# Linear attention and four experts on one core: four more chunks turned without TensorE

## The chip, the cores and the metric

The kernel runs on one core of a Trainium2 chip, in fp32. The time is the device time of one execution in microseconds (us), the median of several runs. A core has five engines with a queue of their own each, which work in order: TensorE (PE: matrix products and transpositions, from on-chip memory SBUF into the 8 banks of PSUM), VectorE (DVE), ScalarE (ACT), GpSimd (POOL) and SyncE (SP), which here only issues DMA transfers. They wait for each other through semaphores. Sixteen DMA engines move the data between DRAM and SBUF, and from DRAM to DRAM.

## The reference

```python
# attention: B=4, H=8, S=768, D=64, block=64; lam: one decay per head
for b in range(S // 64):
    sl = slice(b * 64, (b + 1) * 64)
    qb, kb, vb = q[:, :, sl], k[:, :, sl], v[:, :, sl]
    intra = einsum('bhij,bhjd->bhid', einsum('bhic,bhjc->bhij', qb, kb) * Dmask, vb)
    inter = einsum('bhid,bhde->bhie', qb * lam_pow, kv_state)
    out[:, :, sl] = intra + inter
    kv_state = lam_block * kv_state + einsum('bhsd,bhse->bhde', kb * rev_pow, vb)
x = out.transpose(0, 2, 1, 3).reshape(B * S, H * D)          # 3072 x 512
# four experts: w1 512 x 1024, w2 1024 x 512
p = domain_probs / (domain_probs.sum(-1) + 1e-9)
y = sum(p[:, e:e+1] * (relu(x @ w1[e]) @ w2[e]) for e in range(4))
```

## The kernel before

The 3072 tokens are cut into three groups `g` of 1024, and each group into eight chunks of 128 tokens of one batch entry. Chunks are numbered through: 0 to 7 belong to group 0, 8 to 15 to group 1, 16 to 23 to group 2. In group 1, chunks 8 to 11 are batch entries 0 and 1, chunks 12 to 15 are entries 2 and 3, each with the sequence chunks 2 and 3; group 2 holds the sequence chunks 4 and 5 of all four. A pair of group and expert is a *unit*; twelve units follow each other.

The products with w1 and w2 are done by Strassen's method in the form of Winograd, in two levels: seven products M1 to M7 in place of eight, and within each of them seven again. This needs sums of blocks of x (`x_steps`, `own_x`, `own_x_apart`), of the weights (made by GpSimd, kept in DRAM as `w1_ops`, `w2_sums`, `w2_ops` and read back as `ws_in` and `w2t`), and of the hidden activations (`operands`, `later_operands`).

The main loop runs over the units (`at`), over seven products (`i`) and over eight *slots* (`x`) of a product. In a slot TensorE does a piece of the second product (w2) of this unit, into the banks `q..`, and a piece of the first product (w1) of the next unit, into the banks `g1` and `g3`. Round these pieces everything else is laid out in program order by lists: `lately` (work of the attention for VectorE), `background` (operand sums for VectorE), `own_sums` (sums of x), `adds`, `chores` and `queue` (weight sums on GpSimd and their stores), and `steps`, where the attention of chunks 8 to 23 is placed by `AT`, a list of slot numbers counted through from the loop's start. The functions `tt`, `send` and `vector` keep rough clocks of the engines (`busy`, `moved`, `asked`, `filled`), by which the lists are emptied.

A chunk's attention has these steps. `load_more` loads q and k, `load` v. `turn` brings q and k into the form with the head dimension on partitions. `scores`, at slot `AT`, forms the products of k and q (bank pair `q02`, `q12`) and the new state; `values` of the chunk before, in the same slot, gives that chunk's rows of x, through the score banks `s0` and `s1`. VectorE masks, adds to the state and scales q, by the list `lately`.

There are two ways to turn. On the first, TensorE transposes q and k in eight steps of 128x128 into `s0` and `s1` (line 698), and ScalarE copies both to SBUF (lines 706 and 707). On the second (`comes_across`, `load_across`, `turn_across`), SyncE and ScalarE issue, long before, copies from DRAM to DRAM that move runs of 32 columns into the tensor `across` so that, once loaded, VectorE's transposition of 32x32 blocks (line 678) gives the same form. `bring_across` puts 32 such copies per batch entry into the list `pieces`; `trickle` issues one per slot in the first unit (by SyncE and ScalarE in turn) and one every two slots later on; `load_more` issues what is still missing for its chunk, and then loads. Before the change, the chunks of group 2 go the second way.

A DMA has one of eight semaphores, taken in turn, and the instruction that issues it waits till the last transfer on the same semaphore has landed.

The sums of x for the second unit (`SEQ[1:]`, six times four differences of 128x256) are made in the first unit. `own_x` gives them to VectorE with both operands in SBUF. `own_x_apart`, used before the change for group 2 alone, has ScalarE copy two blocks of 128x256 into a bank first, so that one operand of each difference lies in PSUM; `put_back` then issues the differences.

Of the kernel before, what the change touches and what calls it, by code (L numbers as in the profile page):

```python
# [14 lines left out]
FP32 = mybir.dt.float32  # L15
# [6 lines left out]
def kernel(  # L22
# [36 lines left out]
    C = P  # L59
# [49 lines left out]
    def send(out, in_, by=None):  # L109
        n = 4 * min(packet(out), packet(in_))  # L110
        moved[0] = max(moved[0], now[0]) + 4 * math.prod(out.shape) / n * (9 + n / 25) / 16 / 1714
        if by is None:
            asked[0] = max(asked[0], now[0]) + 0.27
        (by or nc.sync).dma_start(out=out, in_=in_)
# [35 lines left out]
    def where(n):  # L150
        g, x = divmod(n, CPG)
        return (x // 4, x % 4) if g == 0 else (2 * g + x // 2 % 2, 2 * (x // 4) + x % 2)
# [304 lines left out]

    SECOND = NCH - 2  # L460
    across = dram.tile([2, P, NHP, B, 8, 32], FP32, name="across")
    pieces = []

    def bring_across(b):
        for x, of in enumerate((q, k)):
            for y in range(4):
                for ac in range(NHP):
                    src = of[b, 4 * (y // 2) + ac, SECOND * C:, (y % 2) * 32:(y % 2 + 1) * 32]
                    to = across[x, y * 32:(y + 1) * 32, ac, b]
                    pieces.append((b, lambda by, to=to, src=src: send(  # L470
                        out=to, in_=src.rearrange("(t p) d -> p t d", p=32), by=by,
                    )))

    def trickle(m=1, by=None):
        for _ in range(m):
            if pieces:
                pieces.pop(0)[1](by)

    def comes_across(n):
        return where(n)[0] >= SECOND  # L480

    def load_across(n):
        c, b = where(n)
        for x, name in enumerate("qk"):
            t = small(f"{name}x")
            send(
                out=t[:].rearrange("p (h c) -> p h c", c=C),
                in_=across[x, :, :, b, (c - SECOND) * 4:(c - SECOND) * 4 + 4].rearrange("p h t d -> p h (t d)"),
            )
            nat[n, name + "x"] = t  # L490

    def load_more(n):
        if not comes_across(n):
            load(n, "qk")
        else:
            trickle(sum(b <= where(n)[1] for b, _ in pieces))
            load_across(n)
            load(n, "k")

# [125 lines left out]
    def take(queue, force=False):  # L625
        for x, f in enumerate(queue):
            if force or getattr(f, "at", 0) <= now[0] and getattr(f, "can", lambda: True)():
                queue.pop(x)()
                return
# [226 lines left out]
        ))  # L856

    FILL = {1: 18, 2: 43}
    AT = (34, 40, 47, 53, 59, 94, 101, 108, 116, 147, 154, 167, 172, 203, 210, 223)
    steps = []  # L860

    def attention():
# [42 lines left out]
    def later_operands(g, e, m):  # L905

        def step(h, m, a):
            if m == "M4":
                t = h["S2"] = h.pop("S3")
                tt(nc.vector, t[:], a[:], t[:], ALU.subtract)  # L910
            elif m == "M2":
                t = h["S1"] = h.pop("A11")
                tt(nc.vector, t[:], h["S2"][:], t[:], ALU.add)
            else:
                t = h["S4"] = h.pop("A12")
                tt(nc.vector, t[:], t[:], h["S2"][:], ALU.subtract)
                spent(h, "S4")

        def through(hs):
            up = [None] * 4  # L920

            def bring(x):
                up[x] = bank(("q02", "q12")[x % 2], "up")
                nc.scalar.copy(out=up[x][:], in_=hs[x]["A12"][:])

            def less(x):
                t = hs[x]["S4"] = hs[x].pop("A12")
                tt(nc.vector, t[:], up[x][:], hs[x]["S2"][:], ALU.subtract)
                spent(hs[x], "S4")
                if x < 2:  # L930
                    bring(x + 2)

            bring(0)
            bring(1)
            background.extend(lambda x=x: less(x) for x in range(4))

        if m == "M6" and unit_of[g, e] == NEST - 1:
            through([hid[g, e, uu, sj] for sj in (1, 0) for uu in range(2)])
        elif m in ("M4", "M2", "M6"):
            ahead = unit_of[g, e] > 0  # L940
            for by in {"M4": ("M4", "M2")[:1 + ahead], "M2": ("M2",)[ahead:], "M6": ("M6",)}[m]:
                for sj in (1, 0):
                    for uu in range(2):
                        h = hid[g, e, uu, sj]
                        background.append(lambda h=h, by=by, a=h["A22"] if by == "M4" else None: step(h, by, a))
# [598 lines left out]
    def own_x(m, g=0, wait=0):  # L1544

        steps = to_do[m] = []

        def sub(f):
            def step():
                steps.pop()  # L1550
                f()
                if not steps:
                    made.add(("x", g, m))

            steps.append(step)

        for f in x_steps(g, m, nc.vector):
            sub(f)
        own_sums.extend(after(wait, f) for f in steps)
# [202 lines left out]
        lambda: own_weights("M1"), sum_own("S1", "A21", "A22", ALU.add), *w2_steps[0:4], mine["M1"], *w2_steps[4:],  # L1762
        raw["A12"],
    ))
    for b in range(B):
        bring_across(b)
    for m in SEQ0[2:]:
        if m == SEQ0[-1]:
# [42 lines left out]
    for at, (g, e) in enumerate(units):  # L1811
# [14 lines left out]
        for i in range(7):  # L1826
# [36 lines left out]
            turned_back = list(after_last.get(SEQ3[i], ())) if nested and not ahead else []  # L1863
            if at == i == 0:
                for m in SEQ[1:]:
                    own_x(m)
            resting[0] = at == NEST - 1 and i >= 5 or at == NEST and i == 0 or at == NEST - 2 and i == 5
            for x, part in enumerate(order):
                for f in part:
                    if f:  # L1870
                        f()
                now[0] += 1
                put = False
                if nested and ahead:
                    idle[1] = x in (1, 4) and (at - 2 * E + 1, i, x) not in held_at
                    put = put_back()
                added = first_steps.pop((at - 2 * E + 1, i, x), None)
                if added:
                    added()
                all_added(now[0])  # L1880
                if joins and not background:
                    joined()
                elif added and x > 2 or put:
                    pass
                elif (ahead or x % 2 == 0 and x + i) and not (nests and i == 6 and x == 7):
                    if nested or nests:
                        if lately:
                            take(lately)
                        else:
                            rest()  # L1890
                        if at == 2 * E and i in (2, 3) and fits():
                            rest()
                    else:
                        took = False
                        for of in (lately, background, own_sums):
                            if of and (not took or fits() or of is background and len(of) > 4):
                                take(of)
                                took = True
                        if at == 0 and i == 1 and x in (0, 3, 6):
                            take(own_sums)  # L1900
                if nested or nests:
                    take(aside)
                    if own_sums and (nested or fits()):
                        take(own_sums)
                if ending and fits():
                    end_first()
                if nested and ahead and x in (1, 3) and fill3:
                    feed3(*fill3.pop(0))
                if turned_back and x > 0:
                    for y in turned_back.pop(0):  # L1910
                        if SEQ3[i] == END[1]:
                            give(*y[:2], ("s0", "s1"), *y[2:])
                        else:
                            give_across(*y)
                if fill and at * 7 + i >= 6 and x in ((0, 1) if at * 7 + i < 13 else (1, 3, 5) if at * 7 + i == 13 else FEED[nested]):
                    feed(*fill.pop(0))
                while steps and (at * 7 + i) * 8 + x == steps[0][0]:
                    steps.pop(0)[1]()
                if at == 0 or x % 2:
                    trickle(1, nc.scalar if at == 0 and x % 2 else None)  # L1920
                for h in range(1, NG):
                    if x == 3 and 0 <= at * 7 + i - FILL[h] < 7:
                        x_fill(h, SEQ[at * 7 + i - FILL[h]])
                pump(PACE[g])
# [30 lines left out]
```

## Time and profile before

| what | value |
|---|---|
| median of 3 runs (lowest to highest) | 1147.44 us (1145.41 to 1149.49) |
| the profiled execution: its time / its span | 1148.51 us / 1146.7 us |
| mean granted clock of TensorE | 0.999 |
| instructions | 22190 |
| DMA: moved, mean rate | 269.22 MB, 235 GB/s |
| packets: all / under 512 B | 309149 / 141425 |

The span goes from the first to the last instruction. An engine's busy time leaves out its waiting and the issuing of DMAs. In the views, `out<-in` names the tiles written and read; "idle before" is the time that the engine stood still ahead of an instruction, with the one that ended it; a line of code can be that of a helper (117 is `tt`, 114 is `send`). `SPq` rows are DMAs issued by SyncE.

### The profile page before, as it was taken

What the parts mean: (1) busy time and instruction counts of PE and PEld (TensorE: products, weight loads), DVE (VectorE), ACT (ScalarE), POOL (GpSimd) and SP (SyncE); (2) the same over time, 40 slices, a digit from 0 to 9 for tenths busy, and PEclk for the clock granted to TensorE, in tenths of its full rate; (3) what the DMA queues carried; (4) which work ended last, traced back from release to release, by engine and by line L of the source; (5) the groups of instructions that cost most, each with busy time, mean ns of one, the idle gap of its engine ahead of it and who ended that gap; (6) DMA issues with size and microseconds to landing.
All of it is one profiled execution on the core that took longest, in us unless ns stands there. A gap on an engine that the chain in (4) does not pass through costs nothing.

```text
span 1146.7 us, 22190 instructions
## 1 busy us (share of the span) xinstructions
PE 1134.4 (99%) x8015; PEld 989.9 (86%) x8015; DVE 772.9 (67%) x1466; ACT 377.6 (33%) x764; POOL 769.5 (67%) x734
## 2 busy tenths in 40 slices
PE   8999999999999999999999999999999999999998
PEld 7788888888888888888888888888888888888887
DVE  5577876476577748736665566778767576776785
ACT  4322123113312321232344442444345442342332
POOL 2748248645862884853885897895995783873885
PEclk9999999999999999999999999999999999999999
DMA  8785778798999999977767659976679756647552
GB/s 198 169 277 186 192 214 247 253 302 254 304 315 290 280 310 306 299 260 258 244 214 247 199 182 286 339 235 214 207 249 268 225 160 195 201 162 211 173 193 74
DMA packets 309149, 269.22 MB, mean 235 GB/s; under 512 B 141425, under 2 KB 244017, under 8 KB 309041
## 3 DMA queue, kind: packets, MB, share of 16 engines
q1 hardware_dynamic: 291360, 262.66, 74.2%
q10 hardware_dynamic: 17648, 5.15, 2.2%
q8 instruction: 64, 1.05, 0.4%
q14 instruction: 45, 0.36, 0.1%
q0 software_dynamic: 32, 0.00, 0.0%
HBM read 194.83 MB, written 77.10 MB: 237 GB/s over the span
## 4 chain that ended last, share of the span: by engine, by line
PE 94%; DVE 2%; POOL 2%; issue 1%; DMA 1%; ACT 0%; SPq 0%; DVEq 0%; POOLq 0%; ACTq 0%
PE pg L1145 39%; PE pq L1511 23%; PE q L1204 21%; PE pM L1653 3%; PE pc L1653 2%; PE op L795 1%; PE sp L732 1%; PE op L813 1%; PE sp L739 1%; POOL acc L117 1%; PE qp L698 1%; PE pM L1378 1%; PE pg L1511 1%; PE kp L698 1%; DVE m L117 0%
## 5 line engine op out<-in xcount | busy, mean ns | idle before, releaser
L1145 PE MATMUL pg<-xs,ws_in 128*128 128x256 f32 x1960 | 470.5, 380 | 0.5 <-DVE m L117 0.5
L1145 PEld LDWEIGHTS pg<-xs,ws_in 128*128 128x128 f32 x1960 | 370.7, 190 | 53.8 <-DVE m L117 3.3
L117 DVE TENSOR_TENSOR m<-pg,m 128x512 f32<-128x512 f32 x374 | 256.0, 686 | 96.2 <-PE pg L1145 85.0
L1204 PE MATMUL q<-w2t,m 128*128 128x256 f32 x1120 | 265.8, 380 | 1.7 <-issue 1.4
L1204 PEld LDWEIGHTS q<-w2t,m 128*128 128x128 f32 x1120 | 211.5, 190 | 31.6 <-issue 1.8
L117 DVE TENSOR_TENSOR sums<-pq,sums 128x256 f32<-128x256 f32 x272 | 113.2, 421 | 90.3 <-PE pq L1511 78.2
L117 POOL TENSOR_TENSOR m<-m,decay 128x512 f32<-128x512 f32 x91 | 114.5, 1271 | 83.5 <-ACT m L1162 66.5
L1511 PE MATMUL pq<-acc,w2t 128*128 128x256 f32 x688 | 169.2, 379 | 0.0
L1511 PEld LDWEIGHTS pq<-acc,w2t 128*128 128x128 f32 x688 | 130.5, 190 | 18.0
L1162 ACT ACTIVATE m<-m 128x512 f32<-128x512 f32 x99 | 62.4, 630 | 195.3 <-DVE m L117 190.7
L1222 DVE SCALAR_TENSOR_TENSOR acc<-q,gate,acc 128x256 f32<-128x256 f32 x108 | 52.1, 483 | 80.4 <-PE q L1204 79.9
L117 DVE TENSOR_TENSOR m<-m,m 128x512 f32<-128x512 f32 x108 | 91.2, 844 | 6.5 <-ACT m L1128 6.5
L1158 ACT COPY m<-pg 128x512 f32<-128x512 f32 x88 | 51.5, 585 | 133.1 <-PE pg L1145 122.4
L117 POOL TENSOR_TENSOR acc<-hT,hT 128x512 f32<-128x512 f32 x56 | 70.4, 1273 | 22.9 <-DVE hT L117 12.6
L1122 ACT COPY pg<-m 128x512 f32<-128x512 f32 x77 | 45.5, 590 | 113.5 <-DVE m L117 106.1
L117 POOL TENSOR_TENSOR acc<-hT,acc 128x512 f32<-128x512 f32 x56 | 71.2, 1271 | 6.5 <-PE pq L1511 2.7
L1511 PE MATMUL pq<-hT,w2t 128*128 128x256 f32 x288 | 70.0, 379 | 0.0
L117 POOL TENSOR_TENSOR w2o<-w2b 128x512 f32<-128x512 f32 x26 | 34.6, 1355 | 43.2 <-DMA w2b<-in_moe_w_dram 37.7
L1511 PEld LDWEIGHTS pq<-hT,w2t 128*128 128x128 f32 x288 | 54.7, 190 | 7.4
L117 POOL TENSOR_TENSOR kn<-kn,decay 128x512 f32<-128x512 f32 x16 | 17.6, 1098 | 59.9 <-PE kp L698 38.6
L1511 PE MATMUL pq<-m,w2t 128*128 128x256 f32 x228 | 55.4, 379 | 0.0
L1126 ACT COPY m<-pg 128x512 f32<-128x512 f32 x44 | 25.8, 585 | 87.6 <-PE pg L1145 83.4
(157 smaller groups left out, 1468.2 us busy)
## 6 DMA issues: line engine op xcount, KB each, us to landing
w2t<-w_ops SPq DMA_DIRECT2D x129, 256.0 KB, 3.1
ws_in<-w_ops SPq DMA_DIRECT2D x40, 512.0 KB, 4.5
ws_in<-w_ops SPq DMA_DIRECT2D x60, 256.0 KB, 3.5
ws_in<-w_ops SPq DMA_DIRECT2D x40, 384.0 KB, 4.0
w2b<-in_moe_w_dram SPq DMA_DIRECT2D x56, 256.0 KB, 5.0
w_ops<-ops SPq DMA_DIRECT2D x28, 512.0 KB, 4.5
w2t<-w_sums SPq DMA_DIRECT2D x40, 256.0 KB, 4.3
w_sums<-w2o SPq DMA_DIRECT2D x16, 512.0 KB, 4.6
```

Source lines behind the costliest of these rows:

```text
L117: eng.tensor_tensor(out=o, in0=a, in1=b, op=op)
L698: nc.tensor.transpose(out=x[:, ac * C:(ac + 1) * C], in_=y[:, 2 * ac:2 * ac + 2].rearrange("p r d -> p (r d)"), identity=ident[:],)
L732: nc.tensor.matmul(out=sp[r][half[x], ac * BL:(ac + 1) * BL], lhsT=hc(kT)[half[r], ac, blk[x]], rhs=hc(qT)[half[r], ac, blk[x]], start=(ac ...
L1122: nc.scalar.copy(out=banks[tags[1]][:], in_=new["11"][:])
L1126: nc.scalar.copy(out=o[:], in_=p[:])
L1145: nc.tensor.matmul(out=p[:, j * 256:(j + 1) * 256], lhsT=ws[i][:, j * P:(j + 1) * P], rhs=xs[i], start=(fresh and j == 0), stop=True, skip ...
L1158: nc.scalar.copy(out=new[at][:], in_=p[:])
L1162: nc.scalar.activation(out=new[at][:], in_=new[at][:], func=AF.Relu)
L1204: nc.tensor.matmul(out=p[:, s * DH:(s + 1) * DH], lhsT=h[A_OF[m]][:, c * 256 + s * P:c * 256 + (s + 1) * P], rhs=fed2[g, e, m][uu][:, c], ...
L1222: nc.vector.scalar_tensor_tensor(out=o, in0=x, scalar=w, in1=o, op0=ALU.mult, op1=ALU.add)
L1511: nc.tensor.matmul(out=p[:, 0:256], lhsT=fed3[e, m, x // 2][:, x % 2, c * P:(c + 1) * P], rhs=b[B_OF[i]][:, c * 256:(c + 1) * 256], start= ...
L1653: nc.tensor.matmul(out=p[:, s * 256:(s + 1) * 256], lhsT=a[c][:, f:f + P], rhs=b[:, c, j * 256:(j + 1) * 256], start=(s == 0 and c == 0 an ...
```

## The change

Chunks 12 to 15 go the second way too. The tensor `across` now holds the sequence chunks 2 to 5 (16 blocks of 32 rows) in place of 4 and 5 (8 blocks). For batch entries 2 and 3 a copy now takes all four sequence chunks and is twice as large; for entries 0 and 1 it is as before. The order of the copies is by `rank`: entries 2, 3, 0, 1.

The x sums of the second unit are made by `own_x_apart` through the banks `s0` and `s1`, one attempt to take one and one `put_back` in every slot of the first unit. In the first unit the operand sums S1, until now queued at the second product's M2, are queued at M4, as in the other units. In the first product of a unit (`i == 0`) two items of `lately` may be taken in a slot. Four entries of `AT` change: chunk 12 from slot 59 to 58, 13 from 94 to 91, 14 from 101 to 99, 16 from 116 to 115.

```diff
-    SECOND = NCH - 2
-    across = dram.tile([2, P, NHP, B, 8, 32], FP32, name="across")
+    FIRST_ACROSS = CPG + 4
+    across = dram.tile([2, P, NHP, B, 16, 32], FP32, name="across")
     pieces = []
+    rank = {2: 0, 3: 1, 0: 2, 1: 3}

     def bring_across(b):
+        c = min(where(n)[0] for n in range(FIRST_ACROSS, NG * CPG) if where(n)[1] == b)
...
-                    src = of[b, 4 * (y // 2) + ac, SECOND * C:, (y % 2) * 32:(y % 2 + 1) * 32]
-                    to = across[x, y * 32:(y + 1) * 32, ac, b]
-                    pieces.append((b, lambda by, to=to, src=src: send(
+                    src = of[b, 4 * (y // 2) + ac, c * C:, (y % 2) * 32:(y % 2 + 1) * 32]
+                    to = across[x, y * 32:(y + 1) * 32, ac, b, (c - 2) * 4:]
+                    pieces.append((rank[b], lambda by, to=to, src=src: send(
...
     def comes_across(n):
-        return where(n)[0] >= SECOND
+        return n >= FIRST_ACROSS
...
-                in_=across[x, :, :, b, (c - SECOND) * 4:(c - SECOND) * 4 + 4].rearrange("p h t d -> p h (t d)"),
+                in_=across[x, :, :, b, (c - 2) * 4:(c - 1) * 4].rearrange("p h t d -> p h (t d)"),
...
-            trickle(sum(b <= where(n)[1] for b, _ in pieces))
+            trickle(sum(x <= rank[where(n)[1]] for x, _ in pieces))
...
-    AT = (34, 40, 47, 53, 59, 94, 101, 108, 116, 147, 154, 167, 172, 203, 210, 223)
+    AT = (34, 40, 47, 53, 58, 91, 99, 108, 115, 147, 154, 167, 172, 203, 210, 223)
...
-        elif m in ("M4", "M2", "M6"):
-            ahead = unit_of[g, e] > 0
-            for by in {"M4": ("M4", "M2")[:1 + ahead], "M2": ("M2",)[ahead:], "M6": ("M6",)}[m]:
+        elif m in ("M4", "M6"):
+            for by in ("M4", "M2") if m == "M4" else ("M6",):
...
-    for b in range(B):
+    for b in rank:
         bring_across(b)
...
             if at == i == 0:
                 for m in SEQ[1:]:
-                    own_x(m)
+                    own_x_apart(m, g, 0)
...
                 put = False
+                if at == 0:
+                    idle[:] = [("s0", "s1"), i < 3]
+                    put = put_back()
+                    take(own_sums)
...
                                 take(of)
+                                if of is lately and i == 0:
+                                    take(of)
                                 took = True
-                        if at == 0 and i == 1 and x in (0, 3, 6):
-                            take(own_sums)
```

## The prediction

> **What bounds the kernel now.** I read the page's busy times first, then TensorE's waits, then the timeline round the steps that change, and last the DMA share by stretches.
>
> ```profile
> PE 1134.4 (99%) x8015; PEld 989.9 (86%) x8015; DVE 772.9 (67%) x1466; ACT 377.6 (33%) x764; POOL 769.5 (67%) x734
> ```
>
> TensorE (PE) is busy in 1134.4 of 1146.7 us at a granted clock of 0.999. So work taken off TensorE shortens the run by its own time, as long as nothing makes TensorE wait. These are its longest waits (us in total, times, longest):
>
> ```profile
> PE sp L732 <- issue: 1.5, 1, 1.5
> PE q L1204 <- issue: 1.4, 1, 1.4
> PE pg L1145 <- DVE m L117: 1.2, 2, 0.8
> ```
>
> All its waits come to 8.6 us and most lie in the first 50 us. Two of these are in the stretch that changes: 0.8 us of the third line, at 112.39, and the second line, at 203.08.
>
> One turn of a chunk on TensorE, in the timeline (start, length):
>
> ```profile
> 281.04 0.60 PE L698 MATMUL qp<-ident,qn 128*128 128x128 f32 x4
> 281.48 0.60 PE L698 MATMUL kp<-ident,kn 128*128 128x128 f32 x4
> 281.92 1.89 PE L1145 MATMUL pg<-xs,ws_in 128*128 128x256 f32 x8
> ```
>
> From the first transposition's start to the next product's start are 0.88 us. Lengths overlap, so starts count. What takes over (VectorE's and ScalarE's groups; for the tile rows: min/median/max ns, first and last start):
>
> ```profile
> L117 DVE TENSOR_TENSOR xs<-xs 128x256 f32<-128x256 f32 x24 | 18.4, 765 | 0.2
> ```
> ```profile
> L117 DVE TENSOR_TENSOR xs<-xp,xs x28: 414/425/426, 705.8 to 788.6; 128x256 f32<-128x256 f32 x28
> L1578 ACT COPY xp<-xs x14: 577/584/596, 697.1 to 786.0; 128x512 f32<-128x512 f32 x14
> ```
> ```profile
> L678 DVE STREAM_TRANSPOSE qx<-qx x8: 695/702/705, 298.3 to 484.6; 128x512 f32<-128x512 f32 x8
> ```
>
> The same sum costs VectorE 765 ns with both operands in SBUF and 425 ns with one in a PSUM bank. Stretches: length, TensorE, weight loads, VectorE, ScalarE, GpSimd, clock, DMA share, GB/s:
>
> ```profile
> 100.00:120.00 20.00, 19.21 (x89) 16.64 (x88) 16.75 (x25) 4.29 (x8) 17.40 (x18) 1.00 0.75 237
> 190.00:230.00 40.00, 38.58 (x301) 33.59 (x300) 19.72 (x42) 10.38 (x21) 27.32 (x32) 1.00 0.78 252
> 230.00:260.00 30.00, 30.00 (x180) 26.26 (x181) 22.98 (x36) 5.11 (x9) 13.79 (x12) 1.00 0.99 311
> 380.00:480.00 100.00, 99.84 (x903) 87.20 (x902) 68.80 (x127) 23.40 (x53) 72.80 (x84) 1.00 1.00 305
> ```
>
> DMA is full in the last two, and yet TensorE hardly waits: its transfers have time in hand there.
>
> **The change part by part.** The sum is made against the profiled execution's own 1148.5 us (span 1146.7), which lies 1.1 us above the median of 1147.4; I carry the difference over to the median.
>
> *Turns.* Chunks 12 to 15 lose 8 transpositions each: 4 x 0.88 = **3.5 us** off TensorE. The 8 PSUM copies on ScalarE that go (about 0.58 us each) were hidden. VectorE gains 8 transposes of 0.70 us, 1.40 a chunk, where it is busy 49 to 77% (190 to 260). The eight chunks that already go this way show one wait of 0.2 us behind VectorE's state update. Bounds: nothing, and 4 x 0.8 = 3.2 us if each chunk cost the longest VectorE wait of the waits view. I take nothing, from the nearer row.
>
> *Copies in DRAM.* There are 128 as before, but 64 of them twice as large: 32,768 packets of 128 B become 49,152. Over the trace's packet records a packet of 128 B takes 12.9 ns, of 256 B 18.8 and of 512 B 29.5. So 16,384 x 12.9 / 16 engines = 13.2 us of all sixteen are added, the four q loads take away 4,096 x 18.8 / 16 = 4.8, and the loads of the turned chunks add 4,096 x 29.5 / 16 = 7.5. The 13.2 come with the first 64 copies, from 48 to some 160 us, where the share is 0.42 to 0.88; that hides them. The loads come at 175 to 270 us, partly in the full stretch, with 0.7 us net a chunk; matching landings with first uses, the weight tiles there have 4.0 us in hand at 216 and 6.8 at 253. Cost: nothing; bound 16 - 6.8 = 9 us if all of it fell on the one tile with 6.8.
>
> The Trainium skill, "VectorE: DVE Perf Modes", section The three transpose paths, warns that a plain strided DMA copy used as a transpose is 19 times slower than the hardware's path. By that the added copies would take up to 19 x 13.2 = 251 us, an estimate from that page. The trace does not agree for this copy: each packet here is a run of 128 B at 12.9 ns, so the sum stays with the row.
>
> *The queue of SyncE (SP).* This is the step that I trust least. In the built order the copies for batch 1 are now last, and chunk 17's load finds ten still to be issued: they go out in one go ahead of it, and its load of k then waits for all eight DMA semaphores, so for the last of the ten to land. In the kernel before:
>
> ```profile
> 332.22 0.59 SPq L114 DMA_DIRECT2D qx<-across  x1
> 332.86 0.63 SPq L114 DMA_DIRECT2D kx<-across  x1
> 339.11 0.41 SPq L114 DMA_DIRECT2D ws_in<-w_ops  x1
> ```
> ```profile
> 348.84 0.70 DVE L678 STREAM_TRANSPOSE kx<-kx 128x512 f32<-128x512 f32 x1
> ```
>
> Ten issues at 0.56 us put the q load at 337.8. The last copy lands 3.2 to 6.4 us later (rows of 321 to 341 us), so k's load goes out at 341 to 344 and lands, 5.9 us on, at 347 to 350, against a transpose that stands at 348.8. Behind VectorE's wait are queued the sums that free TensorE's banks. Behind the load on SP stand w2 tiles with 21 us in hand and the ws_in at 339.11, landed at 345.0 and used at 356.0: 11.0 us in hand against a delay of 8 to 11, less the 1.45 us of one copy that stood between and now is among the ten. GpSimd's decay of k comes later, at 341.7 before and some 350 now, but it had 14 us of idle time behind it. I take **0.4 us** lost. Bounds: nothing; and with the slowest issue (1.85 us) and landing (8.9) of this copy in the trace, 27 us of delay less 11 in hand, 16 us.
>
> *x sums of the second unit.* 24 sums go from 765 to 425 ns: 8.2 us less on VectorE between 89 and 128 us, a stretch where TensorE waited 0.79 us at 112.39 for a sum stuck behind three of them. I count **0.8 us** gained. Added are 12 ScalarE copies of 0.58 us, 7.0 in all, nearly all within 18 us, where ScalarE was busy 3.5 of 13; each waits for VectorE to free a score bank, and behind it stand the copies that free TensorE's product banks. Following the built order with these lengths, the tightest bank (wanted at 98.49) is freed at about 98.0. Bounds: nothing, and 7.0 us if every copy stood in TensorE's way; I take nothing, as the sums for group 2 go the same way with 2.1 us of waits on ScalarE and none on TensorE.
>
> *S1 sums queued at M4 instead of M2 in the first unit, and two queue items a slot in a product's first round.* They move VectorE work by some slots, hidden in its idle time (3.6 us of 20 at 120 to 140): nothing, bound one wait of 0.8 us.
>
> *Fetch of instructions.* TensorE's three waits for "issue" begin after 1,729, 1,985 and 4,801 of its records in the trace: 256 apart, and 11 times that. The third, **1.4 us** at 203.08, stands just behind chunk 12's burst of 254 records in 1.9 us, which holds one whole block of 256 but for 9 records at its start and 13 after it. In the changed kernel this burst begins 32 records earlier (a turn of 16 gone, one slot of 16 earlier), so a block's edge falls 41 records into it and the next 45 behind it, some 6 us apart; of the twelve later bursts none comes within 18 records of the bad place. I count the 1.4 us as gained; bound nothing.
>
> The Trainium skill, "Runtime: NRT & Kernel Launch", section Instruction fetch mechanics, has blocks of 256 instructions too, but calls their fetch mostly hidden. By that the wait has another cause and stays, and the sum would be 1.4 us higher.
>
> Sum: -3.5 - 0.8 - 1.4 + 0.4 = -5.3 us. That makes 1143.2 for the profiled execution and **1142.1 us** for the median.
>
> **Rivals.**
> - *The fetch wait stays* or moves to another burst: -3.9, 1143.5 us. For it: such waits lie where small instructions are dense, and the kernel keeps 12 bursts; against it: the distances above.
> - *VectorE or ScalarE eats the gain*: four waits of 0.8 us in TensorE's banks, -2.1, 1145.3 us. For it: VectorE at 77% from 230 to 260; against it: the 0.2 us of the eight chunks that go this way.
> - *Slower: the ten copies on SP.* This decides from a delay of 11.0 us on, when the ws_in tile is late; from 16.7 on all gains are gone. With 22 us (halfway between 16.7 and 27) TensorE waits 11: -5.7 + 11 = +5.3, 1152.7 us. For it: DMA is 95% busy from 300 to 380, and ten copies through eight semaphores go at the pace of landings; against it: the copies there were issued in 0.56 to 0.6 us and landed in 3 to 6.
> - *The turns cost nothing now*, because TensorE would have waited anyway: near 1147. Against it: it waits 0.2 us in all round the eight turns of the second group.
>
> **How the numbers follow.** My forecast (1140.5 to 1143.9) gets 0.48, the fetch wait 0.19, the eaten gain 0.17, the slow queue 0.12, turns that cost nothing 0.04. A change of 0.3% is 3.4 us, about what a measurement of this kernel can tell from none, so "faster" ends at 1144.0. Faster: 0.48 and two thirds of the fetch case, 0.61. Same: the rest of it, the eaten gain and the last case, with a little of the slow queue, 0.28. Slower: 0.11. The range goes from 1139.8 (-5.7, and the 2 us by which the fastest run shown lies under the median) to 1147.3, which holds all cases but the slow queue and a few hundredths.
>
> **What would show it.** Right: 96 transpositions at the line of the turns instead of 128 and TensorE busy about 3.5 us less; no wait of TensorE near 112 and none for issue near 200; sums out of xp at 425 ns. Wrong: a wait of k's transpose on DMA near 345, TensorE waiting there for VectorE or for ws_in; ScalarE's product copies late between 90 and 105; a new issue wait behind a later burst; DMA waits of TensorE near 250.

## The result and the profile after

The change made the kernel slower: 1152.27 us (median of 7 runs, 1151.24 to 1154.98) against 1146.78 us before (7 runs, 1144.88 to 1149.49), a ratio of 1.0047 with a 95% interval of 1.0034 to 1.0060. Forecast were 1142.1 us; the time lies above the range. The profiled execution of the changed kernel took 1152.36 us, its span is 1150.6 us, 3.9 more than the 1146.7 of before. Lines of the code have moved by 1 to 2: line 698 is now 700, 732 is 734, 739 is 741, 1145 is 1146.

The busy times of the changed kernel, on its page:

```profile
PE 1131.8 (98%) x7983; PEld 987.5 (86%) x7983; DVE 771.9 (67%) x1474; ACT 379.6 (33%) x768; POOL 768.8 (67%) x734
```

The 32 transpositions are gone (8015 matmuls before) and TensorE is 2.6 us less busy. The gain is more than eaten by one wait. TensorE's waits (us in total, times, longest):

```profile
PE pg L1146 <- POOL ops L117: 8.2, 1, 8.2
PE sp L741 <- issue: 1.9, 2, 1.6
...
PE pg L1146 <- DVE m L117: 0.5, 1, 0.5
PE pg L1146 <- DMA ws_in<-w_ops: 0.2, 1, 0.2
```

The timeline of TensorE round it (start, length):

```profile
99.65 1.03 PE L1146 MATMUL pg<-xs,w1o 128*128 128x256 f32 x4
108.92 2.08 PE L1146 MATMUL pg<-xs,ops 128*128 128x256 f32 x4 [8.25 <-POOL ops L117]
110.79 3.18 PE L1205 MATMUL q<-w2t,m 128*128 128x256 f32 x8
113.81 1.03 PE L1146 MATMUL pg<-xs,ops 128*128 128x256 f32 x4
```

TensorE stands from 100.7 to 108.9 us for `ops`, sums of blocks of w1 that GpSimd makes for the second unit (`own_w1`). Behind the wait it is slow as well: from 108.92 to 113.81 it starts 12 matmuls in 4.89 us. A little later four take 0.86 us (113.81 to 114.67) and eight 1.72 (115.54 to 117.26). The stretches say why (length, TensorE, weight loads, VectorE, ScalarE, GpSimd, clock, DMA share, GB/s):

```profile
104.00:108.00 4.00, 0.00 (x0) 0.00 (x0) 0.00 (x0) 0.00 (x0) 2.29 (x2) 0.50 0.91 325
108.00:112.00 4.00, 3.08 (x7) 2.53 (x8) 0.00 (x0) 0.96 (x2) 3.84 (x6) 0.50 0.81 269
112.00:116.00 4.00, 4.00 (x17) 3.35 (x16) 1.43 (x4) 1.21 (x3) 3.84 (x6) 0.83 0.70 134
116.00:120.00 4.00, 4.00 (x20) 3.54 (x19) 2.43 (x5) 0.59 (x1) 4.00 (x5) 1.00 0.21 35
```

The granted clock falls from 1.00 to 0.50 at 103.2 us, some 2.5 us into the wait, and is back at 1.00 at 113.4, some 4.5 us after its end. The slow starts are another 4.89 - 2.58 = 2.3 us, so the wait costs 10.5 us in all. The Trainium skill, "TensorE: Matmul & The Clock Gate", section What's actually happening, has half the clock after an idle window of about 3.4 us and the full one after as long a busy window. The trace agrees on the two clocks; the drop came after a shorter stand.

Why is `ops` late? GpSimd works in order, and ahead of `ops` stand its four sums of blocks of w2 for expert 1 (`prepare_w2`): T3 = B22 - B12, T1 = B12 - B11, T2 = B22 - T1, T4 = B21 - T2, each to a tile `w2o`, in two halves. GpSimd's timeline, in the kernel before:

```profile
81.99 2.74 POOL L117 TENSOR_TENSOR w2o<-w2b 128x512 f32<-128x512 f32 x2 [6.82 <-DMA w2b<-in_moe_w_dram]
90.23 2.59 POOL L117 TENSOR_TENSOR w2o<-w2b 128x512 f32<-128x512 f32 x2 [5.50 <-DMA w_sums<-w2o]
92.90 5.50 POOL L117 TENSOR_TENSOR w2o<-w2b,w2o 128x512 f32<-128x512 f32 x4
98.48 1.66 POOL L117 TENSOR_TENSOR ops<-w1o 128x256 f32<-128x256 f32 x2
```

and in the changed one:

```profile
83.24 2.50 POOL L117 TENSOR_TENSOR w2o<-w2b 128x512 f32<-128x512 f32 x2 [7.08 <-DMA w2b<-in_moe_w_dram]
97.36 2.51 POOL L117 TENSOR_TENSOR w2o<-w2b 128x512 f32<-128x512 f32 x2 [11.62 <-PE pg L1146]
99.81 2.50 POOL L117 TENSOR_TENSOR w2o<-w2b,w2o 128x512 f32<-128x512 f32 x2
105.71 2.48 POOL L117 TENSOR_TENSOR w2o<-w2b,w2o 128x512 f32<-128x512 f32 x2 [3.39 <-DMA w2b<-in_moe_w_dram]
108.14 1.40 POOL L117 TENSOR_TENSOR ops<-w1o 128x256 f32<-128x256 f32 x2
```

The rows are T3, T1, T2, T4, `ops` (T2 and T4 share a row before). Two things have changed. T1 waits for TensorE till 97.36, where before it waited for a transfer till 90.23. And T4 waits 3.39 us for its block B21.

The second comes from SyncE. The waits of SP from 80 to 100 us, in the changed kernel:

```profile
SPq L114 <- DMA across<-in_k_dram: 11.1, 4, 6.4
```

Of these 11.1 us, 10.6 are three waits for copies that ScalarE issued (the longest 6.4 and 3.8), and 0.6 is one for a copy of SP's own. In the kernel before no wait on an `across` copy stands in that view. Here are SP's and ScalarE's issues in the timeline of the changed kernel:

```profile
84.38 7.17 SPq L114 DMA_DIRECT2D w2t<-w_sums  x2
91.59 0.94 SPq L114 DMA_DIRECT2D w2b<-in_moe_w_dram  x2
96.37 0.34 SPq L114 DMA_DIRECT2D w_sums<-w2o  x1
96.75 3.04 SPq L114 DMA_DIRECT2D across<-in_k_dram  x4
99.84 1.13 SPq L114 DMA_DIRECT2D w2b<-in_moe_w_dram  x2
```
```profile
88.63 0.58 ACT L1159 COPY m<-pg 128x512 f32<-128x512 f32 x1 [0.28 <-PE pg L1146]
88.71 0.67 ACTq L114 DMA_DIRECT2D across<-in_k_dram  x1
91.74 0.58 ACTq L114 DMA_DIRECT2D across<-in_k_dram  x1
```

Between its two `w2t` loads SP stands till the copy that ScalarE issued at 88.71 has landed (91.16), and before `w_sums` till the one of 91.74 has landed (96.31). The eight DMA semaphores are shared by both issuing engines and taken in turn, in the order that the build assumes. In the program before, ScalarE's first copies take their semaphores after SP's run of loads; in the changed one they take them in between. So SP, which had run ahead, now goes at ScalarE's pace, and ScalarE issues between its copies of product banks, at TensorE's pace (the `m<-pg` row ahead of the first). The loads of the blocks of w2 go out at 91.59 and 99.84, where before they went out at 82.79 and 88.84.

The first comes from the buffers. In both programs T1's tile is one of the seven of the pool `stage`. In the program before it got the buffer of T3, which is free when T3 has been copied to DRAM. In the changed one it got that of the first product's `ops`, which TensorE still reads. Nothing in the diff names either. The build places instructions by estimated times and hands out buffers and semaphores by that order; that the doubled copies come in through these estimates is argued, not shown. The run d_copies, below, has both decisions with the copies alone.

A table shows where the 3.9 us lie. It counts matmuls from the start and from the end (worked out from their starts in the traces, us per stretch), with the kernels of the experiments told below:

| kernel | first 1145 | to 1514: holds the wait for `ops` | to 2170 | four turns: to 5000 before the end | to 3000 before the end | rest | span |
|---|---|---|---|---|---|---|---|
| before | 57.7 | 80.7 | 49.7 | 101.2 | 215.5 | 642.1 | 1146.7 |
| d_x | 57.9 | 80.2 | 49.7 | 99.8 | 215.2 | 642.0 | 1144.8 |
| d_t1 | 56.6 | 80.5 | 49.7 | 99.5 | 215.2 | 642.0 | 1143.5 |
| d_pe | 57.6 | 87.8 | 49.7 | 99.8 | 215.2 | 642.0 | 1152.1 |
| after | 55.0 | 90.7 | 49.7 | 96.2 | 216.9 | 642.0 | 1150.6 |
| u_late | 55.2 | 87.2 | 49.7 | 96.2 | 217.2 | 642.0 | 1147.4 |
| u_t1 | 55.0 | 89.3 | 49.7 | 96.2 | 216.4 | 642.0 | 1148.7 |
| u_late_t1 | 57.3 | 80.3 | 49.7 | 96.2 | 215.2 | 642.0 | 1140.7 |
| u_late_t1_x | 58.2 | 80.8 | 49.7 | 96.2 | 217.1 | 642.4 | 1144.4 |

Between the kernel before and the changed one, the second column of times holds 10.0 us of loss and the fifth another 1.5; the fourth holds 5.0 of gain. The first adds 2.6 of gain that the change did not make: the changed kernel and its variants have the same program there and take 55.0 to 58.2 us. It is a difference between executions, and spans of single profiles must be compared without it.

### The profile page after: what moved, and what is told of

Its sections match the earlier page's. It is cut to its first block, busy times and chain, and to the rows that moved or that the text cites. A ratio compares the mean times of both kernels' runs of the same rounds, so it can differ in the third digit from the quotient of the medians.

```text
span 1150.6 us, 22152 instructions
## 1 busy us (share of the span) xinstructions
PE 1131.8 (98%) x7983; PEld 987.5 (86%) x7983; DVE 771.9 (67%) x1474; ACT 379.6 (33%) x768; POOL 768.8 (67%) x734
## 4 chain that ended last, share of the span: by engine, by line
PE 95%; DMA 2%; DVE 2%; issue 1%; ACT 0%; POOL 0%; SPq 0%; DVEq 0%; ACTq 0%; POOLq 0%
PE pg L1146 40%; PE pq L1512 24%; PE q L1205 21%; PE pM L1654 2%; PE pc L1654 2%; PE op L797 1%; PE sp L734 1%; PE op L815 1%; PE sp L741 1%; DMA ws_in<-w_ops 1%; PE pM L1379 1%; DVE m L117 1%; PE pg L1512 1%; DMA w2b<-in_moe_w_dram 0%; PE qp L700 0%
## 5 line engine op out<-in xcount | busy, mean ns | idle before, releaser
L117 DVE TENSOR_TENSOR m<-m,m 128x512 f32<-128x512 f32 x108 | 94.3, 873 | 6.5 <-ACT m L1129 6.5
```

Of the source, the lines that this page charges most:

```text
L117: eng.tensor_tensor(out=o, in0=a, in1=b, op=op)
```

## The experiments

Three theories stood at first. S: SP is held by ScalarE's copies (the semaphores). B: the added bytes of the doubled copies hold up the weights. X: the x sums through the score banks delay something. The ratios are to the kernel before on the same chip. Every kernel here does the whole computation.

**The first copies of the first unit on SP alone (u_late).** From the changed kernel:

```diff
-                    trickle(1, nc.scalar if at == 0 and x % 2 else None)
+                    trickle(1, nc.scalar if at == 0 and i and x % 2 else None)
```

> The changed kernel, with the pieces of the first seven chunk steps of unit 0 issued by SP where half were issued by ScalarE; bytes, copies and x sums unchanged. In its build ScalarE's first piece takes its completion semaphore (of the eight that SP and ScalarE share) only after SP's run to the third w_sums, as in the kernel before. Theory S (SP waits on a semaphore that a ScalarE piece holds, so w2t, w_sums, w2b, GpSimd's own weights and at last TensorE are late): the 8.25 us wait at 108.9 goes and with it the drop of the clock behind it (0.9 us), 1152.3 - 9.1 = 1143.2 us, range 1141.5 to 1145.5. Rival B (the doubled copies hold the DMA engines, and the weights come late for their bytes): the wait stays, 1151 to 1153. Rival X (the x sums through the score banks delay GpSimd or VectorE): the wait stays, 1151 to 1153.

Measured: 1150.06 us, ratio 1.0024 (1.0015 to 1.0033). Only a quarter of what S expected. SP is no longer held: the blocks of w2 are asked for at 83.85 and 92.26. But the wait is still there, of 4.81 us in place of 8.25, and GpSimd's timeline, behind TensorE's row, shows the reason:

```profile
105.49 2.08 PE L1146 MATMUL pg<-xs,ops 128*128 128x256 f32 x4 [4.81 <-POOL ops L117]
```
```profile
97.36 2.50 POOL L117 TENSOR_TENSOR w2o<-w2b 128x512 f32<-128x512 f32 x2 [12.08 <-PE pg L1146]
99.83 4.93 POOL L117 TENSOR_TENSOR w2o<-w2b,w2o 128x512 f32<-128x512 f32 x4
104.72 1.40 POOL L117 TENSOR_TENSOR ops<-w1o 128x256 f32<-128x256 f32 x2
```

T4 comes without a gap now, T1 still waits for TensorE till 97.36. S was a part of it. This is the run that led to T1's buffer, which neither S, B nor X had named.

**The larger copies alone (d_copies).** From the kernel before, with the tensor `across`, the sizes and the order of the copies as in the change, and the turns left on TensorE:

```diff
-    across = dram.tile([2, P, NHP, B, 8, 32], FP32, name="across")
+    across = dram.tile([2, P, NHP, B, 16, 32], FP32, name="across")
...
-                    src = of[b, 4 * (y // 2) + ac, SECOND * C:, (y % 2) * 32:(y % 2 + 1) * 32]
+                    src = of[b, 4 * (y // 2) + ac, c * C:, (y % 2) * 32:(y % 2 + 1) * 32]
...
-    for b in range(B):
+    for b in rank:
```

> The kernel before with the larger copies alone (16 columns of blocks instead of 8, batches in the order 2, 3, 0, 1); the same chunks are turned by TensorE as before, so nothing is saved. The build gives ScalarE's first two pieces the semaphores 3 and 6 between SP's, as in the changed kernel. Theory S: SP is held between its two w2t<-w_sums by some 6 us and TensorE waits about 8 us for ops near 110: 1146.8 + 8.2 + 0.9 = 1156, range 1153 to 1157. Rival B: also slower, by what the bytes cost, 2 to 6 us, with the delay spread over the loads and no hold of SP on a single semaphore. Rival X: 1146.8, range 1146 to 1148.

Measured: 1171.97 us, ratio 1.0229 (1.0204 to 1.0253), far above every expectation. The wait for `ops` is there as expected, with both of its causes in the built program, and so the copies alone, in their new size and order, bring it about; no run parts size from order. Two more waits came with it:

```profile
PE pg L1148 <- POOL ops L117: 8.5, 1, 8.5
PE pq L1514 <- DMA w2t<-w_ops: 6.4, 1, 6.4
PE sp L742 <- DMA qx<-across: 5.3, 1, 5.3
```

The third is named after a load that can't have ended it: TensorE goes on at 375.21, and the `qx` issued last before that, at 371.32, lands at 377.09. What landed just before, at 375.08, on a semaphore that the matmul waits for, is the chunk's `v` (`vn`). SP issues it late, behind the burst of ten copies and the loads and stores that queue up after it:

```profile
345.80 6.90 SPq L114 DMA_DIRECT2D across<-in_k_dram  x10
352.74 0.61 SPq L114 DMA_DIRECT2D qx<-across  x1
368.02 0.37 SPq L114 DMA_DIRECT2D vn<-in_v_dram  x1
```

The changed kernel has the same burst (339.22 to 345.66); the section on the prediction tells what it costs there.

The second, near 790 us, was not followed up.

**The x sums alone (d_x).** From the kernel before:

```diff
-                    own_x(m)
+                    own_x_apart(m, g, 0)
...
+                if at == 0:
+                    idle[:] = [("s0", "s1"), i < 3]
+                    put = put_back()
+                    take(own_sums)
...
-                        if at == 0 and i == 1 and x in (0, 3, 6):
-                            take(own_sums)
```

> The kernel before with the x sums of unit 1 through the score banks alone. The build's semaphore order stays as in the kernel before. Theory S: no wait for ops; the 0.79 us wait at 112 goes: 1146.8 - 0.8 = 1146.0, range 1144.5 to 1147.5. If the 1.42 us of issue at 203 go too: 1144.6. Rival X: TensorE waits some 8 us near 110, 1153 to 1156. Rival B: 1146 to 1147.

Measured: 1146.54 us, ratio 0.9998 (0.9989 to 1.0007). No wait for `ops`, so X falls. TensorE's waits for VectorE at the products go from 1.2 to 0.5 us, as expected, but the medians can't tell 0.8 us from nothing.

**The change without the x sums (u_x).** The same lines the other way round, in the changed kernel.

> The changed kernel with the x sums of unit 1 as before (GpSimd and VectorE through xs<-xs). ScalarE's first pieces keep the semaphores 3 and 6 between SP's. Theory S: the wait for ops stays at about 8 us, and the 0.8 us wait of the x sums may come back or lie inside it: 1152.3, range 1151 to 1154. Rival X: the wait goes, 1143 to 1146. Rival B: 1151 to 1154.

Measured: 1154.26 us, ratio 1.0061 (1.0048 to 1.0075), 0.3 above the range of S and B, with a wait of 8.5 us for `ops`. The wait agrees with S and B and is the second run against X.

After these four, the theory was P: the doubled copies change what the build decides, in two places, T1's buffer and the order of the semaphores, and either alone makes `ops` late.

**Both undone (u_late_t1).** u_late, and for expert 1 the sums T1, T2 and T4 overwrite blocks that no one reads any more, so that they need no new buffer:

```diff
-            t = stage.tile([P, 2, 2, DH], FP32, name="w2o", tag="st")
+            over = {"T1": "B11", "T2": "B22", "T4": "B21"}.get(name) if e == 1 else None
+            t = st[over] if over else stage.tile([P, 2, 2, DH], FP32, name="w2o", tag="st")
```

> The changed kernel with the first seven chunk steps' pieces on SP (as u_late) and, for expert 1 alone, GpSimd's sums T1, T2, T4 of the blocks of w2 written over the blocks B11, B22, B21 and not into new stage buffers. The same bytes and turns as in the changed kernel. Theory P (the doubled copies change what the build decides: T1's stage buffer becomes one that TensorE still reads until 97.36, which costs 4.8 us, and ScalarE's pieces get semaphores between SP's, which costs another 3.4): both are undone, the wait for ops goes, 1150.06 - 4.8 - 0.5 of clock = 1144.8 us, range 1142.5 to 1146. Rival B (bytes of the larger copies): the wait of 4.8 us stays, 1149.5 to 1151.

Measured: 1142.50 us, ratio 0.9960 (0.9946 to 0.9974), faster than both kernels. The wait for `ops` is gone, with the same bytes, copies and turns as in the changed kernel; so B falls as the cause of it. GpSimd's `ops` and TensorE's stretch:

```profile
99.09 1.42 POOL L117 TENSOR_TENSOR ops<-w1o 128x256 f32<-128x256 f32 x2
```
```profile
100.00:120.00 20.00, 20.00 (x94) 17.60 (x94) 11.79 (x25) 6.56 (x12) 15.55 (x18) 1.00 0.90 251
```

The changed kernel had 11.75 us of TensorE at a clock of 0.74 in this stretch.

**The buffer alone undone (u_t1).** The same lines in the changed kernel, with ScalarE's copies as they are there.

> The changed kernel with T1, T2, T4 of expert 1 in place, ScalarE's pieces as in the changed kernel. Theory P: SP still stands from 85 to 91 and again to 96 for ScalarE's pieces, the last block B21 of w2 is asked for at 99.8 and lands near 105, so T4 and ops are as late as before: the wait stays at 7.5 to 8.3 us, 1152, range 1150.5 to 1153. If the buffer is the whole cause: 1143 to 1145. Rival B: 1151 to 1153.

Measured: 1151.26 us, ratio 1.0039 (1.0026 to 1.0053); inside the range; the wait is 6.5 us, below the expected 7.5 to 8.3. GpSimd waits for its blocks now:

```profile
95.21 4.96 POOL L117 TENSOR_TENSOR w2b<-w2b 128x512 f32<-128x512 f32 x4 [10.47 <-DMA w2b<-in_moe_w_dram]
104.03 2.48 POOL L117 TENSOR_TENSOR w2b<-w2b 128x512 f32<-128x512 f32 x2 [3.86 <-DMA w2b<-in_moe_w_dram]
106.47 1.40 POOL L117 TENSOR_TENSOR ops<-w1o 128x256 f32<-128x256 f32 x2
```
```profile
107.24 2.08 PE L1147 MATMUL pg<-xs,ops 128*128 128x256 f32 x4 [6.54 <-POOL ops L117]
```

With u_late this closes a square: both causes 8.25 us, the buffer alone 4.81, the semaphores alone 6.54, neither 0. They don't add up, since both hold up the same chain and the later one ends it. With SP held, the later one is T4's wait for its block, with T1's buffer or without. The block is asked for at 99.84 in the changed kernel and at 99.86 here, but T4 starts at 105.71 there and at 104.03 here; the 1.7 us between the two waits are this difference in landing, and the medians of the two kernels (ratios 1.0047 and 1.0039) are not told apart. In the changed kernel it is thus the semaphores that set the wait, and the buffer alone would make one too.

**The buffer alone, in the kernel before (d_pe).** T1 is written over the `ops` tile of the first own product; nothing else in the code differs from the kernel before.

```diff
-            t = stage.tile([P, 2, 2, DH], FP32, name="w2o", tag="st")
+            at_pe = e == 1 and name == "T1"
+            t = used[-1][:].rearrange("p (u c) d -> p u c d", u=2) if at_pe else stage.tile([P, 2, 2, DH], FP32, name="w2o", tag="st")
```

(`used` holds the `ops` tiles of `own_w1`.)

> The kernel before with one thing changed: GpSimd writes expert 1's T1 into the stage buffer of the ops tile of the first own product, which TensorE reads until about 97. No copy, turn or x sum differs from the kernel before. Theory P: T1 moves from 90.2 to about 97.5 us, ops from 98.5 to 105, TensorE waits some 4.8 us for ops at 105 and its clock drops for some us: 1146.9 + 4.8 + 0.5 = 1152, range 1150.5 to 1153. Rival B: no change, 1146 to 1147.5.

Measured: 1153.70 us, ratio 1.0050 (1.0036 to 1.0064), 0.7 above the range and as slow as the changed kernel. SP asks for the blocks at 83.61 and 88.87, as in the kernel before; GpSimd waits for TensorE, and TensorE for GpSimd:

```profile
93.56 1.27 POOL L117 TENSOR_TENSOR ops<-w2b 128x512 f32<-128x512 f32 x1 [7.95 <-PE pg L1148]
99.55 1.50 POOL L117 TENSOR_TENSOR ops<-w2b 128x512 f32<-128x512 f32 x1 [4.72 <-PE pg L1148]
```
```profile
107.23 2.08 PE L1148 MATMUL pg<-xs,ops 128*128 128x256 f32 x4 [4.31 <-POOL ops L117]
109.10 3.19 PE L1207 MATMUL q<-w2t,m 128*128 128x256 f32 x7
```

One buffer, with no transfer touched, is enough for a loss of this size. Its wait is shorter than in the changed kernel, 4.31 us and the slow clock behind it, but no turns are saved here.

**The control (d_t1).** The lines of u_late_t1 in the kernel before.

> The kernel before with T1, T2, T4 of expert 1 in place: the control for the two runs in place. T1 need not wait for the copy of T3 to DRAM any more and comes some 2 us sooner, but TensorE does not wait for ops in the kernel before: 1146.9, range 1145.5 to 1148, by every theory.

Measured: 1146.90 us, ratio 0.9998 (0.9986 to 1.0011). Writing in place gains nothing by itself, so u_late_t1 is not faster for that.

**The turns alone (u_late_t1_x).** u_late_t1 with the x sums as before.

> The four turns alone, clear of the build's two choices: u_late_t1 with the x sums of unit 1 as in the kernel before. By the prediction's terms the turns take 4 x 0.88 = 3.5 us from TensorE and the ten copies ahead of chunk 17 give back 0.4: 1147 - 3.1 = 1143.9 us, range 1142.5 to 1145, with no wait for ops and TensorE's wait of 0.8 us for an x sum near 111 back. If a turn on TensorE costs only half of its span because other work fills it: 1145.5. The x sums would then be worth what lies between this run and u_late_t1, 0.8 to 1.5 us.

Measured: 1146.12 us, ratio 0.9999 (0.9982 to 1.0017), against the expectation. Yet the stretch with the four turns is 96.2 us in its trace as in u_late_t1, and most of what it lies above u_late_t1 stands in the first 1145 matmuls (58.2 us) and between 5000 and 3000 before the end (217.1). There, 0.7 us are waits for VectorE and 0.6 are two waits that the view calls "issue", at line 742. So both went to the chip once more, side by side (labels u_late_t1_again and u_late_t1_x_again).

> u_late_t1 once more, beside its sister without the x sums on the same chip. In the traces the stretch from 2170 matmuls after the start to 5000 before the end, which holds the four turns, takes 99.5 to 99.8 us in three kernels that turn on TensorE and 96.2 in every kernel that does not; the first 1145 matmuls take 55.0 to 58.2 us in kernels whose code is the same there. If the medians follow the stretches: 1142.5, range 1141.5 to 1144.

> u_late_t1_x once more on the same chip as u_late_t1. If the four turns are worth what their stretch shows (3.4 us) and the 1146.12 of the first time came from the start and from waits for nothing that the profile shows: 1143.5, range 1142.5 to 1145, about 0.5 to 1 above its sister. If the x sums are worth 3 us or more that no stretch shows: 1146, 3 above its sister.

Measured: 1143.18 us, ratio 0.9974 (0.9962 to 0.9986), and 1144.57 us, ratio 0.9980 (0.9968 to 0.9992). The turns alone make the kernel faster in this measurement, though not in the first one, whose interval overlaps with it. Side by side, what the x sums add is not told apart from nothing.

**The burst ahead of chunk 17 spread out (u_spread).** From u_late_t1:

```diff
-                if at == 0 or x % 2:
+                if at <= 1 or x % 2:
```

> u_late_t1 with SP's pieces in the next expert's steps at every step and not at every other, so that no ten copies stand ahead of chunk 17's load. By the prediction's term of 0.4 us for them: 1142.5 - 0.4 = 1142.1 us, range 1141 to 1143.5, with the slack of the weights' loads around 350 us back. If the burst costs nothing on this path: 1142.5. If the denser pieces hold up SP's weight loads between 150 and 250 us instead: 1144 or more, with waits for DMA at L1147 there.

Measured: 1154.50 us, ratio 1.0055 (1.0035 to 1.0076): the third case. TensorE's waits from 230 to 320 us:

```profile
PE pg L1147 <- DMA ws_in<-w_ops: 4.9, 3, 2.2
PE pg L1147 <- DMA ws_in<-in_moe_w_dram: 1.7, 1, 1.7
```

The copies stand between weight loads that seem to have little time in hand there; whether SP's time or the copies' bytes make the loads late was not tested. In one burst, as they were, they cost far less: u_late_t1 has no wait of TensorE behind them above 0.2 us.

## Why the prediction was wrong, point by point

- *Copies in DRAM: "Cost: nothing".* The step that failed. The bytes did cost nothing, as reasoned: u_late_t1 moves all of them without a wait. What the step left out is that a copy twice as long moves the built program's order. T3 stands 75 places later in it against the other engines' instructions, T1 gets a buffer that TensorE reads, and ScalarE's copies get semaphores between SP's. TensorE then waits 8.25 us for `ops` and is slow behind it, 10.5 us in all, where the prediction had nothing and 9 us as its bound. It asked of SP only what stands behind the burst at chunk 17, and it did not compare what each instruction of the two programs waits for. GpSimd's order round T1 is the same in both kernels; a wait of T1 on TensorE is new. The 251 us set beside this term don't follow: they multiply 13.2 us, which is already worked out from the measured time of such packets of these copies.
- *Turns: 3.5 us.* Right. The stretch with the four turns takes 99.5 to 99.8 us in three kernels with the turns on TensorE (d_x, d_t1, d_pe) and 96.2 in those without (96.6 in u_late_t1_again; u_spread has its waits for DMA there): 2.9 to 3.6. VectorE's added transposes cost nothing there.
- *Fetch of instructions: 1.4 us gained.* The place was right, the gain was not. In the fourteen traces every wait for "issue" above 0.2 us and up to 310 us begins after 449, 1,473, 1,729, 1,985, 4,801 or 6,593 of TensorE's records, whole blocks of 256 apart, as the prediction read it from three of them. But at such a place there is a wait in some executions and not in others. d_x, d_t1 and d_pe send TensorE through the same matmuls in the same order as the kernel before and have no wait at 4,801; d_copies has one of 0.9. The row was read as a property of the code, and it was one draw. What makes these waits long or short stays open.
- *x sums: 0.8 us gained.* The wait at 112.39 is gone in d_x, but it is also gone where T1 is in place and the x sums are as before, so what it hung on stays open. The medians show no gain. ScalarE's copies cost nothing, as said.
- *The queue of SP: 0.4 us lost.* Too small in this trace. The load that it named cost about that: ws_in waits 0.25 us at 358.26, and nothing in u_late_t1. But behind the burst SP also issues the next chunk's `v` later, which the prediction did not look at. These are the load and the matmul that uses it, in the kernel before and in the changed one:

```profile
358.43 0.55 SPq L114 DMA_DIRECT2D vn<-in_v_dram  x1
371.86 0.63 PE L739 MATMUL sp<-vn,kn 64*64 64x64 f32 x16
```
```profile
369.36 0.38 SPq L114 DMA_DIRECT2D vn<-in_v_dram  x1
375.92 0.68 PE L741 MATMUL sp<-vn,kn 64*64 64x64 f32 x16 [1.55 <-issue]
```

  The view says "issue", but the semaphore instruction ahead of this matmul ends at 375.87, just when the last part of `v` has landed (375.83), and the place is no block's edge in TensorE's records. So the term was 1.8 us here. Six of the eight traces of kernels with the burst and without the four turns show this wait, 0.3 to 1.6 us; u_spread, which has no burst, has none there; that the burst makes it was not tested by itself. The slow rival had the right sign and, with 1152.7 us, nearly the time, but that is luck: it wanted 11 us from SP's queue at 340 us, and the loss came between 85 and 109 us, by way of SP and GpSimd.
- *The sum.* -5.3 us were forecast; u_late_t1, which is the change without the two decisions of the build, took 0.9960 and 0.9974 of the time before, that is 3 to 4.6 us less. Without the 1.4 us for the fetch the sum would have been -3.9, which is the rival of the fetch wait that stays or moves.

## What to carry to other kernels

When a change alters the size or number of transfers, compare the two programs by what each instruction waits for, on the engines that the change doesn't touch as well: a buffer or a semaphore that the build hands out differently can cost more than the change gains (10.5 us here against 3.4). Two engines that issue DMAs and share the completion semaphores are tied to each other's pace; here it helped to let the engine of the loads issue the copies that are not urgent while the loads run ahead (u_late). Sums that overwrite an operand that no one else reads any more need no new buffer, so the build can't give them one that is still read. And when a wait is put down to "issue" or to an odd load, look at the semaphore instruction ahead of it and at what lands when it ends.

## What the runs showed of the hardware

- After TensorE's waits of 4.3 to 8.5 us for `ops` in six kernels, matmuls of 128x256 started every 0.43 us in place of 0.22, and the clock was back 2.9 to 5.2 us after the wait's end. In u_spread a wait of 2.15 us was followed by 4 us at a clock of 0.57, shorter than the idle window that the Trainium skill's page gives. A wait has this price on top.
- The Trainium skill, "Trainium Kernel Development and Optimization", section Key Constraints, says that issuing DMAs from several engines at once only saves issue time. Here it also held one engine for the other: SP stood 10.6 us on copies that ScalarE issued.
- TensorE's waits for "issue" above 0.2 us and up to 310 us began in the fourteen traces at one place in blocks of 256 of its records (193 past a multiple of 256) and took 0.3 to 2.1 us; at the same place of the same order some executions had none.
- The first 1145 matmuls took 55.0 to 58.2 us in single executions of the changed kernel and its variants, whose program is the same there. That is about half as wide as the spread between the runs of one of them (1141.31 to 1147.51 us in u_late_t1_x_again).
